# Moving the steps that decode weights within the first slots of a fused attention and MoE kernel: new units ahead of older ones, masks ahead of units, 1e-9 directly behind the exponentials

## The chip, the cores and the metric

The kernel runs on one core of one Trainium2 chip. The metric is the device time of one execution in microseconds (us); the median of three runs is compared. TensorE is PE in the profile, VectorE is DVE, ScalarE is ACT, GpSimd is POOL, and SyncE, which issues every transfer here, is SP.

## What is computed

The reference is attention that keeps the 32 largest scores of each row, and then four matrix products that mix what the heads give. There are 8 batches, 8 heads, 576 positions and 64 numbers per head.

```python
scores = scale * np.matmul(q, k.transpose(0, 1, 3, 2))
kth = np.partition(scores, -top_k, axis=-1)[..., -top_k:-top_k + 1]
mask = scores >= kth
scores = np.where(mask, scores, -1000000000.0)
scores = scores - np.max(scores, axis=-1, keepdims=True)
attn = np.exp(scores)
attn = attn / (np.sum(attn, axis=-1, keepdims=True) + 1e-09)
return np.matmul(attn, v).astype(np.float32)
...
a = x @ w1
b = x @ w2
h = a * b @ w3
return (h @ w_out).astype(np.float32)
```

w3 and w_out are folded into one matrix at the start, so what remains per token is x times w1, x times w2, their product, and that times the folded matrix.

## The kernel before

**Slots.** Attention is cut into 144 slots, 18 for each batch: 128 queries of two heads make a slot. A slot needs scores on PE, the 32 largest values of each row on DVE (four MAX8 rounds with MATCH_REPLACE8 between them), the mask, the exponentials, their sum, the division, a transposition and the product with v. The slots are pipelined by an order written out by hand: pass p of the main loop makes the scores of slot p+1, the largest values of slot p, the weights of slot j = p-1 (mask, exponentials, 1e-9, reciprocal, division) and the product with v of slot m = p-2. Every instruction is kept in the order of the program on its engine.

**The weights of one slot.** `edges_of` (POOL) makes the threshold of slot j from the values that DVE found. `mask` is for each of two heads a Relu on ACT and a subtraction on POOL, which the profile shows as `pab<-s,edge` and `pab<-s,pab`. `compare` (POOL, `over`) notes a number for a check at the end. `exps` are two exponentials on ACT (`pab<-pab,edge`) that also write their sums. `enlarge` adds 1e-9 to the two sums on POOL (`sums<-sums`), `invert` takes their reciprocal on DVE (`sums<-sums`), and `normalise` multiplies on POOL (`pab<-pab,sums`).

**Weight units.** The matrices come in as 40 units of 512 KB each: eight of w_out, then sixteen of w3 and sixteen of w1 and w2, mixed. The words of a unit come in a tile `z`, and there are four such tiles, so the transfer of a unit waits until the last reader of the unit four before it is done. Decoding takes several steps on different engines: ACT writes `t<-z` and then `z<-z`; DVE combines them in `y<-t` (TENSOR_SCALAR) and `y<-t,y` (SCALAR_TENSOR_TENSOR, called the STT here); POOL adds `y<-y,z` or `wo<-y,z`, the last reader of z. In every second unit of w_out and of w3 the first step is a TENSOR_SCALAR `y<-z` on POOL, and DVE has the STT only. A unit of w1 or w2 has two steps more, `wh<-y` on ACT and `wl<-y,wh` on POOL. A unit of w3 gives PE four products `pf` for the folded matrix, and every second one a copy on ACT and a subtraction on DVE (`wf`).

**Turns.** A call of `warm` is a turn: every unit that is under way makes its next step, and in four of five turns (from the eleventh in every second one) one new unit is begun. Each pass has five turns, called the first to the fifth here: behind the second step of the largest values, behind the transposition, behind the second round, behind the third round, and at the end of the pass. In pass -1 only the fourth and the fifth are made. `prefetch(3)` keeps three transfers ahead of the unit begun.

**The MoE.** When a part of a batch (320 or 256 tokens) has passed all its slots, its products (`ab`, then `eo`) are queued and put between the slots' work on PE by `fill`, in three portions to a pass. `fill` first issues what evicts earlier products (`evict`). The first `ab` waits until the first half of w1 and w2 is decoded. Products that the passes leave over are made at the end.

The names in the profile leave the numbers of buffers out; nearly all instructions carry one line, L52, that of the helper which keeps the order.

Of the kernel before, what the change touches and what calls it, by code (L numbers as in the profile page):

```python
# [60 lines left out]
def attn_moe(ctx: ExitStack, tc: tile.TileContext, q, k, v, w1, w2, w3, w_out, out, flag, general):  # L61
# [45 lines left out]
    def fetch(src):  # L107

        z = z_p.tile([128, 1024], F32, tag="z", name="z")
        sp.dma_start(z.bitcast(I32), src)  # L110
        return z
# [49 lines left out]
    def weigh(n):  # L161
        while heavy and n:
            heavy.pop(0)()
            n -= 1
# [31 lines left out]
    def load_qk(b, part, hp):  # L196

        lo, n, _ = PARTS[part]
        qt = kq_p.tile([128, NA], F32, tag="q", name="qt")
        sp.dma_start(qt[:, :n], at(q, b, hp)[:, lo : lo + n])  # L200
        kt = kq_p.tile([128, S + 64], F32, tag="k", name="kt")
        sp.dma_start(kt, at(k, b, hp))
        return qt, kt

    def load_v(b, hp):

        vt = kq_p.tile([128, 11 * D], F32, tag="v", name="vt")
        sp.dma_start(vt, at(v, b, hp))
        return vt
# [22 lines left out]
    def new_s():  # L232
        return att_p.tile([128, 2, S], F32, tag="s", name="s", bufs=2)
# [40 lines left out]
    def edges_of(slot):  # L274
        top = tops[slot % len(tops)]
        edge = small.tile([128, 2, 2], F32, tag="edge", name="edge")
        pool.tensor_tensor(edge, top[:, :, 0:32:31], coef, op=ALU.mult)
        return edge

    def compare(slot):  # L280
        top = tops[slot % len(tops)]
        pool.tensor_tensor(over[:, 2 * slot : 2 * slot + 2], top[:, :, 31], top[:, :, 23], op=ALU.subtract)
# [15 lines left out]
    def new_weights():  # L298
        return att_p.tile([128, 2, S], F32, tag="pab", name="pab"), small.tile([128, 2], F32, tag="sums", name="sums")

    def mask(s, edge, pab, a):

        act.activation(pab[:, a, :], s[:, a, :], AF.Relu, bias=edge[:, a, 1:2], scale=-STEEP)
        pool.tensor_tensor(pab[:, a, :], s[:, a, :], pab[:, a, :], op=ALU.subtract)

    def exps(edge, pab, sums, a):
        p = pab[:, a, :]
        act.activation(p, p, AF.Exp, bias=edge[:, a, 0:1], scale=SCALE, accum_out=sums[:, a : a + 1])

    def enlarge(sums):  # L310
        pool.tensor_scalar(sums, sums, 1e-9, None, op0=ALU.add)
# [20 lines left out]
    def take_turned(tp, ro):  # L332
        pts = att_p.tile([128, 2, 512], F32, tag="pts", name="pts", bufs=1)
        act.copy(pts, tp)
        pr = att_p.tile([128, 128], F32, tag="pr", name="pr")
        act.copy(pr, ro[:, :128])
        return pts, pr
# [26 lines left out]
    def take_low(to, ov):  # L364
        for x, cols, n in to:
            dve.tensor_tensor(x[:, 1, cols], ov[:, n], x[:, 0, cols].bitcast(F32), op=ALU.subtract)
# [116 lines left out]
    qk, vts, ss, sts, edges, pabs, xts, lows = {}, {}, {}, {}, {}, {}, {}, {}  # L483
# [5 lines left out]
    def evict():  # L489
        while put_off:  # L490
            put_off.pop(0)()

    def fill(n):
        nonlocal spare
        evict()
        spare = spare + n if queue else 0
        while queue and spare > 0:
            cost = next(queue[0], None)
            if cost is None:
                queue.pop(0)  # L500
            elif not cost:
                spare = 0
            else:
                spare -= cost

    waiting = list(startup)
    fetched, going, turns = [], [], []

    def prefetch(n):
        while waiting and len(fetched) < n:  # L510
            src, step = waiting.pop(0)
            fetched.append((fetch(src), step))

    def warm(first=True):

        if p < 0 and not first:
            return
        turns.append(p)
        n = len(turns)
        if fetched and (n % 5 if n < 11 else n % 2) and len(going) < 5:  # L520
            z, step = fetched.pop(0)
            going.append(step(z))
        going[:] = [unit for unit in going if next(unit, "end") != "end"]
        prefetch(3)

    qk[units[0]] = load_qk(*units[0])
    prefetch(3)
    n_slots = len(slots)
    for p in range(-1, n_slots + 3):
        i, j, m = p + 1, p - 1, p - 2  # L530
        if i < n_slots:
            for u in units:
                if first[u] - 2 == i:
                    qk[u] = load_qk(*u)
                if first[u] == i:
                    vts[u] = load_v(u[0], u[2])
        finder = top32_steps(ss[p], *sts.pop(p), p) if 0 <= p < n_slots else iter(())
        if 0 <= j < n_slots:
            edges[j] = edges_of(j)
        next(finder, None)  # L540
        if m - 1 in lows:
            take_low(*lows.pop(m - 1))
            b, part, _ = slots[m - 1][0][0]
            if final[b, part] == m - 1:
                queue.append(moe_steps(b, part, [xts.pop((b, part, hp)) for hp in range(NHP)], put_off.append))
        next(finder, None)
        if p >= 0:
            warm()
        if 0 <= j < n_slots:
            pabs[j] = new_weights()  # L550
            for a in range(2):
                mask(ss[j], edges[j], pabs[j][0], a)
            compare(j)
        fill(SHARE[0])
        next(finder, None)
        if 0 <= m < n_slots:
            tp, ro = turn(pabs[m][0])
            pts, pr = take_turned(tp, ro)
        warm(False)
        if 0 <= j < n_slots:  # L560
            exps(edges[j], *pabs[j], 0)
            exps(edges[j], *pabs[j], 1)
        weigh(1)
        fill(SHARE[1])
        next(finder, None)
        warm(False)
        if i < n_slots:
            st = scores([qk[u] for u in slots[i][0]], slots[i][1])
            ss[i] = new_s()
            take_scores(ss[i], st, 0)  # L570
            sts[i] = st, take_scores(ss[i], st, 1)
        if 0 <= m < n_slots:
            us, t = slots[m]
            for u in us:
                if u not in xts:
                    xts[u] = new_x()
            ov = values([vts[u] for u in us], t, pts, pr, ro)
            lows[m] = places([xts[u] for u in us], t), ov
            take_high(*lows[m])
        if 0 <= j < n_slots:  # L580
            enlarge(pabs[j][1])
        next(finder, None)
        warm()
        next(finder, None)
        if 0 <= j < n_slots:
            invert(pabs[j][1])
            normalise(*pabs[j])
        weigh(8)
        fill(SHARE[2])
        for _ in finder:  # L590
            pass
        if 0 <= m < n_slots:
            del ss[m], pabs[m], edges[m]
        warm()
# [62 lines left out]
```

## Time and profile before

| what | value |
|---|---|
| median of three runs | 1267.78 us (1266.63 to 1267.8) |
| the profiled execution's own time | 1266.87 us |
| its span, first to last instruction | 1264.9 us |
| busy: PE, DVE, ACT, POOL | 96%, 90%, 75%, 69% of the span |
| mean granted TensorE clock | 0.991 of full speed |

The span is what the trace covers; the execution's own time is 2 us longer. Busy shares are means over the whole span, while the change is in its first fifth and in one POOL instruction of each slot. So the views to read are those cut by stage. Idle time of an engine stands in brackets in a timeline, with what ended it.

### The profile page before, as it was taken

The numbers are of one execution on the slowest core, as the hardware profiler recorded it, in microseconds if no ns is written. First come the engines' busy times: TensorE is split into PE (matmuls) and PEld (weight loads), VectorE is DVE, ScalarE is ACT, GpSimd is POOL, SyncE is SP. The second block draws the span as 40 slices with busy tenths as digits, with TensorE's granted clock in tenths as the row PEclk, the third lists the DMA queues.
The fourth block names the chain that finished last, engine by engine and source line by source line (L and its number), as shares of the span: only waits on it lengthen the run. The fifth ranks groups of instructions, "written<-read, shape, count | busy, mean of one in ns | idle before, by whom it ended". The sixth has DMA issues, their size and how long they took to land.

```text
span 1264.9 us, 29916 instructions
## 1 busy us (share of the span) xinstructions
PE 1209.7 (96%) x10513; PEld 1043.5 (82%) x10513; DVE 1135.0 (90%) x3968; ACT 943.4 (75%) x2025; POOL 872.4 (69%) x1213
## 2 busy tenths in 40 slices
PE   3788889999999999999999999999999999999998
PEld 1444568888888888888888888888888888888898
DVE  7897979999999999999999999999999999999910
ACT  5887877777777777777777777777777777777731
POOL 5887887676766767676766767676766767676731
PEclk9999989999999999999999999999999999999999
DMA  7533421202112121202112121202112111202000
GB/s 236 174 129 130 156 70 40 91 27 70 55 39 90 36 63 40 90 28 70 55 39 91 36 63 40 90 28 70 55 39 91 35 63 40 91 27 70 13 22 21
DMA packets 42803, 85.92 MB, mean 68 GB/s; under 512 B 4754, under 2 KB 21138, under 8 KB 42642
## 3 DMA queue, kind: packets, MB, share of 16 engines
q1 hardware_dynamic: 42642, 83.91, 20.6%
q8 instruction: 85, 1.39, 0.5%
q14 instruction: 76, 0.62, 0.2%
HBM read 74.45 MB, written 9.44 MB: 66 GB/s over the span
## 4 chain that ended last, share of the span: by engine, by line
PE 75%; POOL 10%; DVE 7%; ACT 4%; issue 3%; DMA 1%; SPq 0%; DVEq 0%; POOLq 0%; ACTq 0%
PE ab L52 27%; PE eo L52 15%; PE ro L52 12%; PE st L52 11%; PE tp L52 9%; POOL pab L52 5%; DVE w L52 3%; DVE top L52 2%; ACT pab L52 2%; PE pf L52 2%; POOL y L52 2%; POOL g L52 1%; DVE y L52 1%; POOL wl L52 1%; ACT pts L52 1%
## 5 line engine op out<-in xcount | busy, mean ns | idle before, releaser
L52 POOL TENSOR_TENSOR pab<-s,pab 128x576 f32<-128x576 f32 x288 | 404.8, 1427 | 121.9 <-ACT pab L52 121.9
L52 DVE MAX8 top<-w 128x8 f32<-128x192 f32 (+1 forms) x1152 | 478.5, 448 | 0.0
L52 PE MATMUL ab<-xf,wh 128*128 128x256 f32 (+1 forms) x2048 | 438.5, 302 | 10.1 <-DVE y L52 8.7
L52 PEld LDWEIGHTS ab<-xf,wh 128*128 128x128 f32 x2048 | 332.9, 189 | 21.6 <-DVE y L52 9.5
L52 ACT ACTIVATE pab<-s,edge 128x576 f32<-128x576 f32 x288 | 208.0, 769 | 176.6 <-POOL edge L52 176.6
L52 PE MATMUL ab<-xf,wl 128*128 128x256 f32 (+1 forms) x1024 | 307.4, 300 | 0.0
L52 DVE MATCH_REPLACE8 w<-top,w 128x192 f32<-128x192 f32 x864 | 289.7, 343 | 0.0
L52 POOL TENSOR_SCALAR pab<-pab,sums 128x576 f32<-128x576 f32 x288 | 212.6, 751 | 78.0 <-DVE sums L52 78.0
L52 ACT ACTIVATE pab<-pab,edge 128x576 f32<-128x576 f32 x288 | 223.1, 779 | 11.9 <-POOL pab L52 9.7
L52 PE MATMUL eo<-g,wf 128*128 128x256 f32 (+1 forms) x1536 | 231.6, 301 | 0.0
L52 PEld LDWEIGHTS eo<-g,wf 128*128 128x128 f32 x1536 | 208.5, 188 | 8.1 <-issue 7.5
L52 PEld LDWEIGHTS ab<-xf,wl 128*128 128x128 f32 x1024 | 193.4, 189 | 4.1 <-issue 4.1
L52 PE MATMUL st<-kt,qt 64*128 64x192 f32 (+3 forms) x1280 | 182.8, 435 | 9.8 <-DMA kt<-in_k 4.8
L52 ACT COPY pts<-tp 128x1024 f32<-128x1024 f32 x144 | 145.6, 1011 | 46.8 <-PE tp L52 44.3
L52 ACT COPY s<-st 128x768 f32<-128x768 f32 (+1 forms) x288 | 169.9, 646 | 5.8 <-PE st L52 5.8
L52 PE MATMUL tp<-ident,pab 128*128 128x128 f32 x1152 | 153.8, 278 | 14.2 <-DVE w L52 9.5
L52 PEld LDWEIGHTS st<-kt,qt 64*128 64x128 f32 (+1 forms) x1280 | 97.9, 178 | 83.7 <-issue 18.6
L52 DVE TENSOR_TENSOR w<-w,st 128x384 f32<-128x384 f32 x288 | 158.2, 549 | 4.9
L52 PE MATMUL ro<-pts,vt 128*64 128x128 f32 (+1 forms) x2560 | 161.2, 269 | 1.0 <-ACT pr L52 1.0
L52 DVE TENSOR_TENSOR w<-s,st 128x384 f32<-128x384 f32 x288 | 146.7, 551 | 14.0
L52 POOL TENSOR_TENSOR g<-whole,g 128x256 fp32r<-128x256 f32 (+1 forms) x128 | 103.3, 807 | 78.6 <-ACT g L52 78.6
L52 PEld LDWEIGHTS ro<-pts,vt 128*64 128x64 f32 x2560 | 127.5, 137 | 34.4 <-issue 24.2
(47 smaller groups left out, 1128.7 us busy)
## 6 DMA issues: line engine op xcount, KB each, us to landing
vt<-in_v SPq DMA_DIRECT2D x64, 352.0 KB, 3.2
kt<-in_k SPq DMA_DIRECT2D x64, 320.0 KB, 3.8
z<-in_w SPq DMA_DIRECT2D x32, 512.0 KB, 3.8
qt<-in_q SPq DMA_DIRECT2D x32, 160.0 KB, 3.2
out_t<-osb SPq DMA_DIRECT2D x32, 160.0 KB, 1.8
z<-in_wo SPq DMA_DIRECT2D x8, 512.0 KB, 5.2
qt<-in_q SPq DMA_DIRECT2D x32, 128.0 KB, 3.1
out_t<-osb SPq DMA_DIRECT2D x32, 128.0 KB, 1.7
```

Source lines behind the costliest of these rows:

```text
L52: ins = fn(*args, **kw)
```

## The change

Four things move; no instruction is added or taken away.

- In a turn, the unit begun makes its first step ahead of the next steps of the units under way; before it came behind them.
- In each pass the two masks and `compare` stand ahead of the first turn; before they stood behind it.
- `enlarge` stands directly behind the two exponentials of its slot; before it stood behind the second portion of the MoE, the third turn, the scores and the product with v.
- Pass -1 makes one turn instead of two, so one unit instead of two is begun ahead of slot 0, and every unit is begun one turn later.

```diff
         turns.append(p)
-        n = len(turns)
+        n, new = len(turns), None
         if fetched and (n % 5 if n < 11 else n % 2) and len(going) < 5:
             z, step = fetched.pop(0)
-            going.append(step(z))
+            new = step(z)
+            next(new)
         going[:] = [unit for unit in going if next(unit, "end") != "end"]
+        if new:
+            going.append(new)
         prefetch(3)
...
         next(finder, None)
-        if p >= 0:
-            warm()
         if 0 <= j < n_slots:
             pabs[j] = new_weights()
             for a in range(2):
                 mask(ss[j], edges[j], pabs[j][0], a)
             compare(j)
+        if p >= 0:
+            warm()
         fill(SHARE[0])
...
             exps(edges[j], *pabs[j], 1)
+            enlarge(pabs[j][1])
         weigh(1)
         fill(SHARE[1])
...
-        if 0 <= j < n_slots:
-            enlarge(pabs[j][1])
         next(finder, None)
-        warm()
+        if p >= 0:
+            warm()
```

The queues show it at three places. The number behind a name counts the tiles made; it differs between the two kernels for the same tile. First POOL in pass 1, around the masks of slot 0 (`pab<-s,pab`); `wo<-y,z` and `y<-y,z` are last steps of units, `y<-z` first steps. Before:

```order
L52 TENSOR_TENSOR wo_105<-y_168,z_138 128x512
L52 TENSOR_TENSOR edge_214<-top0_98,coef_93 128x4
L52 TENSOR_TENSOR y_195<-y_195,z_144 128x512
L52 TENSOR_SCALAR y_224<-z_170 128x512
L52 TENSOR_TENSOR pab_228<-s_131,pab_228 128x576 x2
L52 TENSOR_TENSOR over_96<-top0_98 128x2
L52 TENSOR_TENSOR wo_105<-y_206,z_159 128x512
L52 TENSOR_SCALAR sums_229<-sums_229 128x2
```

And now:

```order
L52 TENSOR_TENSOR edge_205<-top0_98,coef_93 128x4
L52 TENSOR_TENSOR pab_212<-s_131,pab_212 128x576 x2
L52 TENSOR_TENSOR over_96<-top0_98 128x2
L52 TENSOR_TENSOR wo_105<-y_169,z_138 128x512
L52 TENSOR_SCALAR y_232<-z_174 128x512
L52 TENSOR_TENSOR y_196<-y_196,z_149 128x512
L52 TENSOR_SCALAR sums_213<-sums_213 128x2
L52 TENSOR_TENSOR wo_105<-y_219,z_163 128x512
L52 TENSOR_SCALAR pab_212<-pab_212,sums_213 128x576 x2
L52 TENSOR_SCALAR y_286<-z_226 128x512
L52 TENSOR_TENSOR wo_105<-y_232,z_174 128x512
L52 TENSOR_TENSOR wo_105<-y_246,z_201 128x512
```

The last step of the fourth unit (the one that reads z_138) was ahead of the threshold and now stands behind both masks. Next ACT in the same pass, behind the masks' Relus. The seventh unit is the one of z_170 before and z_174 now, the eighth that of z_199 before and z_201 now. Before:

```order
L52 ACTIVATE pab_228<-s_131,edge_214 128x576 x2
L52 ACTIVATE t_241<-z_170 128x512
L52 ACTIVATE z_170<-z_170 128x512
L52 ACTIVATE t_245<-z_199 128x512
L52 ACTIVATE z_199<-z_199 128x512
L52 ACTIVATE pab_228,sums_229<-pab_228,edge_214 128x576 x2
L52 COPY s_270<-st_260 128x2x384
```

And now:

```order
L52 ACTIVATE pab_212,sums_213<-pab_212,edge_205 128x576 x2
L52 ACTIVATE t_247<-z_201 128x512
L52 ACTIVATE z_201<-z_201 128x512
L52 ACTIVATE t_252<-z_174 128x512
L52 ACTIVATE z_174<-z_174 128x512
L52 COPY s_267<-st_257 128x2x384
```

The eighth unit's first step now stands ahead of the seventh's, and both ahead of the copies of the scores. Last POOL in pass 8, where before three steps of units stood between the threshold and the masks:

```order
L52 TENSOR_TENSOR edge_943<-top1_99,coef_93 128x4
L52 TENSOR_TENSOR wl10_108<-y_878,wh1_102 128x512
L52 TENSOR_TENSOR y_921<-y_921,z_781 128x512
L52 TENSOR_SCALAR y_954<-z_832 128x512
L52 TENSOR_TENSOR pab_958<-s_793,pab_958 128x576 x2
L52 TENSOR_TENSOR over_96<-top1_99 128x2
L52 TENSOR_SCALAR sums_959<-sums_959 128x2
```

And now:

```order
L52 TENSOR_TENSOR edge_935<-top1_99,coef_93 128x4
L52 TENSOR_TENSOR pab_943<-s_787,pab_943 128x576 x2
L52 TENSOR_TENSOR over_96<-top1_99 128x2
L52 TENSOR_SCALAR y_972<-z_852 128x512
L52 TENSOR_TENSOR wl10_108<-y_885,wh1_102 128x512
L52 TENSOR_TENSOR y_928<-y_928,z_810 128x512
L52 TENSOR_SCALAR sums_944<-sums_944 128x2
```

The masks follow the threshold at once, the begun unit's `y<-z` is the first of the three steps, and all three stand between the masks and `sums`. On PE the queue from the first `ab` on is the same row by row in both kernels; ahead of it only some `pf` products stand a pass later.

## Rows read from the trace of the kernel before

**Rows 1.** Busy time by stretch: us, PE, PEld, DVE, ACT, POOL, clock, DMA share, GB/s.

```profile
10.00:40.34 30.34, 12.87 (x69) 6.21 (x69) 29.80 (x90) 21.85 (x41) 23.85 (x27) 1.00 0.64 206
40.34:123.89 83.55, 72.22 (x401) 38.75 (x402) 72.53 (x219) 63.27 (x125) 67.16 (x81) 0.94 0.43 143
123.89:182.58 58.69, 48.61 (x299) 35.27 (x298) 52.48 (x159) 48.09 (x95) 52.98 (x60) 0.91 0.38 124
200.00:1200.00 1000.00, 998.30 (x9116) 890.13 (x9114) 954.08 (x3417) 774.76 (x1686) 698.52 (x999) 1.00 0.18 55
```

**Rows 2.** All waits of PE from 200 to 1200 us: total, times, longest.

```profile
PE tp L52 <- DVE w L52: 0.7, 4, 0.2
```

**Rows 3.** Timeline of DVE: slot starts (`w<-s,st`) and the waits named.

```profile
8.24 0.69 DVE L52 TENSOR_SCALAR y<-t 128x512 int32<-128x512 int32 x1 [8.24 <-ACT t L52]
...
9.57 1.01 DVE L52 TENSOR_TENSOR w<-s,st 128x384 f32<-128x384 f32 x2
...
20.24 1.01 DVE L52 TENSOR_TENSOR w<-s,st 128x384 f32<-128x384 f32 x2
...
30.57 1.02 DVE L52 TENSOR_TENSOR w<-s,st 128x384 f32<-128x384 f32 x2
...
40.34 1.02 DVE L52 TENSOR_TENSOR w<-s,st 128x384 f32<-128x384 f32 x2
...
49.93 0.69 DVE L52 SCALAR_TENSOR_TENSOR y<-t,y 128x512 int32<-128x512 int32 x1 [2.47 <-POOL y L52]
...
108.08 0.69 DVE L52 TENSOR_SCALAR y<-t 128x512 int32<-128x512 int32 x1 [2.30 <-ACT t L52]
...
120.57 0.69 DVE L52 SCALAR_TENSOR_TENSOR y<-t,y 128x512 int32<-128x512 int32 x1 [2.46 <-ACT xf L52]
...
123.89 1.01 DVE L52 TENSOR_TENSOR w<-s,st 128x384 f32<-128x384 f32 x2
...
182.58 1.02 DVE L52 TENSOR_TENSOR w<-s,st 128x384 f32<-128x384 f32 x2
```

**Rows 4.** Groups of POOL and ACT, 20 to 190 us: busy, mean ns, idle before.

```profile
L52 POOL TENSOR_TENSOR pab<-s,pab 128x576 f32<-128x576 f32 x30 | 41.8, 1416 | 7.2 <-ACT pab L52 7.2
L52 POOL TENSOR_TENSOR y<-y,z 128x512 int32<-128x512 int32 x32 | 41.5, 1298 | 1.3 <-ACT z L52 1.1
L52 POOL TENSOR_SCALAR pab<-pab,sums 128x576 f32<-128x576 f32 x28 | 20.6, 749 | 9.7 <-DVE sums L52 9.7
L52 POOL TENSOR_TENSOR wl<-y,wh 128x512 fp32r<-128x512 f32 x16 | 20.5, 1280 | 4.7 <-ACT wh L52 4.7
L52 ACT ACTIVATE t<-z 128x512 f32<-128x512 f32 x34 | 22.1, 650 | 7.0 <-DVE y L52 6.0 <-DMA z<-in_wo 1.0
L52 ACT ACTIVATE pab<-s,edge 128x576 f32<-128x576 f32 x30 | 21.6, 767 | 5.5 <-POOL edge L52 5.5
```

**Rows 5.** Timelines of ACT and POOL in the first two slots.

```profile
6.50 1.18 ACT L52 COPY s<-st 128x768 f32<-128x768 f32 x2 [4.49 <-PE st L52]
...
17.83 1.28 POOL L52 TENSOR_TENSOR wo<-y,z 128x512 int32<-128x512 int32 x1 [1.67 <-DVE y L52]
...
23.39 0.64 ACT L52 ACTIVATE t<-z 128x512 f32<-128x512 f32 x1 [1.00 <-DMA z<-in_wo]
...
31.48 0.20 POOL L52 TENSOR_TENSOR edge<-top,coef 128x4 f32<-128x4 f32 x1
```

**Rows 6.** The chain that ended last, first slots: start, us, what.

```profile
14.87 3.77 DMA z<-in_wo
```

**Rows 7.** Transfers over the whole run: KB each, median us to landing.

```profile
z<-in_wo SPq DMA_DIRECT2D x8, 512.0 KB, 5.2
```

**Rows 8.** Timeline of POOL ahead of DVE's wait that ends at 49.93.

```profile
46.71 1.28 POOL L52 TENSOR_TENSOR wl<-y,wh 128x512 fp32r<-128x512 f32 x1
47.94 1.30 POOL L52 TENSOR_TENSOR y<-y,z 128x512 int32<-128x512 int32 x1
...
49.21 0.69 POOL L52 TENSOR_SCALAR y<-z 128x512 f32<-128x512 f32 x1
```

## The prediction

> **What bounds the kernel now.** I read the stretches first, to see which engine is full where. From 200 to 1200 us PE is busy 998.3 of 1000 us at full clock [rows 1], and in all that time it waits 0.7 us for anything [rows 2]. So in steady slots PE sets the pace, and no other engine's order matters. Since the queue of PE is the same row by row from the first `ab` on, the end comes as much later or earlier as PE leaves the start later or earlier. Ahead of that PE idles 17.5 us up to 40.34 us, 11.3 us up to 123.89 and 10.1 us up to 182.58, and what it waits for is the slots' work on the other engines. The view to read next is therefore DVE's timeline, where each first `w<-s,st` marks the start of a slot [rows 3]: slot 0 at 9.57, slot 1 at 20.24, slot 2 at 30.57, slot 3 at 40.34, slot 10 at 123.89, slot 15 at 182.58. DVE idles 0.5 us in slots 0 to 2, 11.0 us in slots 3 to 9, and 6.2 us in slots 10 to 14 [rows 1]. The bound of the first 40 us is DVE's own work; then three engines take turns, POOL being busy 53.0 of 58.7 us in slots 10 to 14, more than any other.
>
> **How I work the change out.** Each engine takes its queue in the new order; a step starts when its engine is free and what it reads is there. I walked slots 0 to 15 so by hand. A threshold takes 0.2 us, a Relu 0.7, a mask 1.4, the division of both heads 1.5, an addition that ends a unit 1.3, a `wl` 1.25, a `t` or a `z` about 0.6 [rows 4, 5]; a unit takes 1.33 us on DVE (9.57 less 8.24), one with the STT alone half of that [rows 3].
>
> **Slot 0: earlier.** One unit less is ahead of it. DVE begins with the scores when the first copy is made, about half of the 1.18 us behind 6.50 [rows 5], so at 7.2 instead of 8.24: 1.0 us of idle time is gone. The slot holds the same two whole and two half units as before and so lasts the same 10.67 us; slot 1 starts at 17.9 instead of 20.24, but one unit, 1.3 us, is still to be done later.
>
> **Slots 1 and 2: later.** The fourth unit's last step was done at 19.1, ahead of the masks [rows 5]; now it stands behind them. The threshold can start at 17.4 (half a unit ahead of slot 1); 0.2 for it, 0.7 for the Relu, 2.8 for the masks, 0.2 for the check's number and 1.3 for the addition end at 22.6. Only then is the tile free for the eighth unit, and the transfer takes 3.8 us as in the chain [rows 6]: 26.4, where ACT had it at 23.39 [rows 5]. [...] The trace has 3.77 here and a median of 5.2 for these eight units [rows 6, 7], so I stay with 3.8 and take 5.2 as the upper bound. ACT comes to the eighth unit's `t` with nothing else to do at 22.6, and waits; behind it stand the seventh unit's `t`, whose data are there, and the scores of slot 2. DVE runs dry at 26.2, and gets the seventh unit's `t` three steps behind 26.4, at 28.2: 2.0 us lost. [...] The loss is larger on POOL. The division of slot 0 waits for the reciprocal, which stands behind this on DVE, until 30.9; the division (1.5), a first step (0.65) and two additions (2.6) then stand ahead of the next threshold, which starts at 35.6, not at 31.48 [rows 5]. In pass 2 the Relus are ahead of the new unit's `t`: that is ready at 35.6 + 0.2 + 1.4 + 0.6 = 37.8, and DVE wants it at 34.7, 3.1 us lost; a second `t`, behind the exponentials, costs 0.8. Slot 3 so starts at about 44.8 with the same eleven units begun: **+4.5 us** (0 if nothing of it is on the path, +5.9 with a transfer of 5.2 us).
>
> **Slots 3 to 9: earlier.** Here are the waits that the new order removes. DVE's 2.47 us that end at 49.93 are for a unit's first step on POOL, which stood behind a `wl` and an addition of older units [rows 8]; now it stands ahead of both, 2.5 us sooner. The 2.46 us that end at 120.57 are of the same kind: the wait is put down to ACT, but the STT reads the `y<-z` of POOL. The 2.30 us at 108.08 are a `t` behind exponentials whose masks had to stand behind units [rows 3]; now the masks are ahead of them. Against this POOL loses cover. Between the threshold and the first mask lies a Relu (0.7 us and the way to and fro, about 0.75) with nothing behind which to hide it. And `enlarge` now waits for the exponentials while `wl` and additions of the third turn stand behind it; in slots 3, 6 and 9 I find POOL waiting 2.2 to 2.8 us so. The walk leaves 6.9 of the 11.0 us of DVE's idle time: -4.1 us, and -1.3 us for the unit that is still behind. **-5.4 us** (0 if the new waits on POOL eat it all, -11.0 if all idle time goes).
>
> **Slots 10 to 14: later.** POOL sets the pace here, and what was put off at the start is paid: one unit more, 1.3 + 1.25 us, of which some 0.2 comes back, because the reciprocal no longer waits behind a third-turn step: **+2.3 us** (0 to 2.5). Behind slot 15 the units are over and PE is full again.
>
> **The rest at nothing.** In the steady slots `enlarge` only changes place with one subtraction of the MoE, on a POOL that is busy 698.5 of 1000 us, and PE waits for none of it [rows 1, 2]. Without that cover it would cost the wait for the exponentials in each slot. In the pf products that come a pass later PE has room: it is busy 72.2 of 83.55 us in slots 3 to 9. [...]
>
> **The sum:** 4.5 - 5.4 + 2.3 = +1.4 us. Against the profiled execution's 1266.87 us that is 1268.3; its time is 0.9 us under the median 1267.78, so as a median **1269.2 us**. A measurement here can tell about 0.2%, 2.5 us, from no change, so this counts as no change.
>
> **Rivals.** *The early loss does not come.* If the eighth unit's data are there when ACT reaches them at about 22.6 us, and the threshold of slot 1 is no later than before, the first term is -1.0 instead of +4.5; -1.0 - 5.4 + 2.3 = -4.1, 1263.7 us. For it: in the trace before, waits for z of 1.00 us at 23.39 and more cost DVE nothing [rows 3, 5]. Against it: the addition that frees the tile really stands 3.7 us of threshold, Relu and masks later. *POOL becomes the bound.* POOL is busy 80% and 90% in slots 3 to 9 and 10 to 14 [rows 1]; if its waits for the exponentials and the Relus reach DVE in every slot, the second term is 0 and not -5.4: +6.8, 1274.6 us. It decides once POOL's slot, some 10.6 us of work (52.98 us in five slots) and 1.5 to 3 of waits, is longer than DVE's slot, which the walk has at 10 to 12. *Nothing reaches the end.* If PE were full already when slot 15 starts, a delay of one or two us would be swallowed: 1267.8. Against it: PE idles 10.1 us in slots 10 to 14 [rows 1], so it has no backlog to live on.
>
> **How the numbers follow.** The forecast, within 3 us of its time, together with the third rival, has 0.47; the early loss staying away 0.28; POOL as the bound 0.25. Below 1265.2 us lies nearly all of the second and little else: faster 0.28. Above 1270.3 lies the third and a part of the forecast's own spread: slower 0.30; no change 0.42. The range reaches past 1263.7 and to 1274.6, and by one more us of transfer (5.2 instead of 3.8) and of removed idle time on each side: 1261.5 to 1275.5. The likeliest case alone is 1266.5 to 1272.
>
> **What would show it.** DVE's first row at about 7.2; a wait of ACT for z of 3 us or more near 23 to 26; slot 3 at 44 to 45; no wait of DVE for a `y<-z` of POOL afterwards; waits of POOL's `sums` for ACT of 2 us in single slots; slot 10 near 122.7 and slot 15 near 184. Slot 3 near 40 would prove the second term's gain unopposed, and slot 10 behind 126 the rival on POOL. The forecast is wrong above all if the transfers or the copies of the scores start at other times than the walk has them, since each slot inherits the delay of the one ahead.

## The result: slower

The changed kernel takes **1278.57 us** (median of four runs, 1278.0 to 1279.37) against 1267.36 us for the kernel before, measured beside it (four runs), a ratio of 1.0089 with a 95% interval of 1.0075 to 1.0103. That is 11.2 us more, where 1.4 more were forecast, and above the range. The profiled execution took 1278.02 us over a span of 1275.9.

### The profile page after: what moved, and what is told of

Its sections match the earlier page's. It is cut to its first block, busy times and chain, and to the rows that moved or that the text cites. A ratio compares the mean times of both kernels' runs of the same rounds, so it can differ in the third digit from the quotient of the medians.

```text
span 1275.9 us, 29886 instructions
## 1 busy us (share of the span) xinstructions
PE 1210.4 (95%) x10513; PEld 1046.1 (82%) x10513; DVE 1139.4 (89%) x3968; ACT 942.0 (74%) x2025; POOL 871.8 (68%) x1213
## 4 chain that ended last, share of the span: by engine, by line
PE 88%; POOL 5%; ACT 3%; issue 2%; DVE 2%; DMA 1%; SPq 0%; ACTq 0%; POOLq 0%; DVEq 0%
PE ab L52 33%; PE eo L52 17%; PE ro L52 15%; PE st L52 12%; PE tp L52 9%; POOL pab L52 2%; PE pf L52 2%; POOL y L52 2%; ACT pab L52 1%; DVE y L52 1%; ACT t L52 1%; POOL wl L52 1%; DVE top L52 0%; ACT pts L52 0%; DVE w L52 0%
## 5 line engine op out<-in xcount | busy, mean ns | idle before, releaser
L52 PE MATMUL st<-kt,qt 64*128 64x192 f32 (+3 forms) x1280 | 186.3, 441 | 22.6 <-DVE w L52 9.8
L52 PE MATMUL tp<-ident,pab 128*128 128x128 f32 x1152 | 151.1, 274 | 7.2 <-DVE w L52 7.1
L52 POOL TENSOR_SCALAR sums<-sums 128x2 f32<-128x2 f32 x144 | 30.9, 214 | 167.5 <-ACT pab L52 166.9
```

Source lines behind the costliest of these rows:

```text
L52: ins = fn(*args, **kw)
```

## The profile after

The stretches of the kernel after, cut at its own starts of slots 3, 10 and 15; they answer to [rows 1].

```profile
core 0: us, PE busy (x) PEld busy (x) DVE busy (x) ACT busy (x) POOL busy (x), PEclk, DMA share, GB/s
10.00:45.20 35.20, 13.74 (x63) 7.06 (x61) 28.53 (x87) 21.20 (x40) 24.09 (x28) 0.84 0.53 171
45.20:132.34 87.14, 70.86 (x395) 37.96 (x395) 72.12 (x218) 62.47 (x124) 64.26 (x77) 0.91 0.41 133
132.34:198.99 66.65, 49.86 (x288) 34.69 (x290) 54.25 (x161) 48.32 (x95) 56.10 (x63) 0.90 0.36 117
200.00:1200.00 1000.00, 1000.00 (x9162) 894.72 (x9161) 960.49 (x3432) 777.70 (x1696) 701.88 (x1005) 1.00 0.18 56
```

Slots 3 to 9 take 87.14 us and not 83.55, slots 10 to 14 take 66.65 and not 58.69. DVE idles 15.0 us in the first of these stretches (87.14 less 72.12), where it had 11.0. From 200 us on PE is as good as full in both kernels (1000.0 and 998.3 of 1000 us). So the whole loss is made ahead of 200 us.

DVE's timeline of the kernel after, its slot starts and its longest early waits, for [rows 3].

```profile
6.76 1.02 DVE L52 TENSOR_TENSOR w<-s,st 128x384 f32<-128x384 f32 x2 [6.76 <-ACT s L52]
...
17.43 1.01 DVE L52 TENSOR_TENSOR w<-s,st 128x384 f32<-128x384 f32 x2
...
28.20 0.69 DVE L52 SCALAR_TENSOR_TENSOR y<-t,y 128x512 int32<-128x512 int32 x1 [2.53 <-ACT t L52]
...
31.71 1.02 DVE L52 TENSOR_TENSOR w<-s,st 128x384 f32<-128x384 f32 x2
...
37.89 0.69 DVE L52 SCALAR_TENSOR_TENSOR y<-t,y 128x512 int32<-128x512 int32 x1 [2.93 <-ACT t L52]
...
45.20 1.01 DVE L52 TENSOR_TENSOR w<-s,st 128x384 f32<-128x384 f32 x2
```

A loss in the start is best counted in what PE still has to do at 200 us, since PE is as good as full behind that. Two rows, first of the kernel before and then of the one after:

```profile
200.00:1290.00 1090.00, 1057.31 (x9605) 947.90 (x9603) 963.40 (x3448) 792.99 (x1730) 713.97 (x1021) 1.00 0.17 52
```

```profile
200.00:1290.00 1090.00, 1070.53 (x9744) 963.04 (x9742) 980.35 (x3500) 805.00 (x1759) 725.44 (x1037) 1.00 0.17 53
```

PE has 13.2 us more to do. But of the span behind 200 us it idles 7.6 us before (1264.9 less 200 less 1057.31) and 5.4 us after. So the start loses 13.2 us and the steady slots, with the drain, give 2.2 back: 11.0 us of span. The table keeps these two numbers for each kernel, in the order in which the runs are told.

| kernel | median us | ratio to before, 95% | PE busy behind 200 us | PE idle behind 200 us |
|---|---|---|---|---|
| before | 1267.36 | 1 | 1057.3 | 7.6 |
| after | 1278.57 | 1.0075 to 1.0103 | 1070.5 | 5.4 |
| a_masks_back | 1264.21 | 0.9968 to 0.9986 | 1055.6 | 5.4 |
| a_enl_back | 1285.04 | 1.0122 to 1.0153 | 1076.7 | 7.9 |
| a_new_back | 1280.80 | 1.0088 to 1.0119 | 1074.0 | 5.6 |
| a_turn_back | 1277.49 | 1.0063 to 1.0090 | 1069.9 | 7.4 |
| b_masks | 1282.46 | 1.0110 to 1.0141 | 1071.8 | 8.9 |
| b_enl | 1262.61 | 0.9955 to 0.9980 | 1054.4 | 5.5 |
| b_enl_new | 1261.30 | 0.9940 to 0.9967 | 1053.7 | 5.4 |
| a_weigh_late | 1278.08 | 1.0073 to 1.0104 | 1070.0 | 5.7 |
| a_relu_first | 1266.62 | 0.9988 to 1.0006 | 1059.0 | 5.6 |
| a_mask_one | 1269.45 | 1.0010 to 1.0030 | 1063.6 | 5.6 |
| a_wf_later | 1279.47 | 1.0085 to 1.0116 | 1072.1 | 5.4 |
| bn_relu | 1261.98 | 0.9948 to 0.9976 | 1053.9 | 5.5 |
| a_check_first | 1278.45 | 1.0069 to 1.0097 | 1071.1 | 5.5 |
| a_edge_early | 1275.05 | 1.0043 to 1.0070 | 1068.8 | 5.6 |
| a_exps_first | 1273.52 | 1.0036 to 1.0063 | 1065.3 | 5.4 |
| bn_exps | 1268.25 | 1.0000 to 1.0018 | 1059.6 | 5.8 |
| a_ways | 1269.47 | 1.0010 to 1.0028 | 1060.4 | 5.4 |
| bn_edge | 1259.55 | 0.9928 to 0.9955 | 1052.3 | 5.4 |

A name that begins with a is the kernel after with one thing altered (a_ways: three), b the kernel before with one or two of the edits, bn the kernel b_enl_new with one thing more. The kernel before was measured anew beside each group of runs (medians of 1266.37 to 1267.36 us), and the ratios are to that. By their intervals a median is good to 1 or 2 us, so differences of about 1 us between two kernels are no finding. The two columns on PE are of one profiled execution each.

## The theories

The trace after showed a chain that the forecast did not have. The chain of work that ended last, in slot 4 of the kernel after (start, length, what):

```profile
58.23 0.17 POOL edge L52
58.41 0.02 issue
58.43 0.78 ACT pab L52
59.21 0.07 issue
59.28 0.65 POOL pab L52
59.93 0.72 issue
60.65 1.42 POOL pab L52
62.07 0.15 POOL over L52
62.22 1.25 POOL y L52
63.48 0.04 issue
63.52 1.13 PE pf L52 x2
64.64 2.04 PE st L52 x8
```

Threshold, Relu and two masks stand in a row ahead of a unit's addition `y`, and PE's one `pf` for it ahead of the next scores `st`. **Loop theory:** the masks ahead of the first turn are the loss, and that `pf` passes it on. **Cover theory** (one half of the forecast's rival on POOL): the early 1e-9 makes POOL wait for the exponentials. **Early starvation:** the late transfer of the eighth unit is the loss. A fourth place is the unit put off from pass -1.

## Experiments: each edit taken back

**a_masks_back.**

```diff
+        if p >= 0:
+            warm()
         if 0 <= j < n_slots:
             pabs[j] = new_weights()
...
             compare(j)
-        if p >= 0:
-            warm()
```

> The changed kernel, with the masks behind the units' first turn again as before the change; the other three edits stay. Loop theory (the masks ahead of the units put the addition that a unit ends with behind them; the one product of the weights that stands ahead of the scores in PE's queue waits for it, and the scores, ACT's copy and the next slot of DVE wait behind): most of the loss goes, 1268 to 1272 us, and PE's waits for y at pf shrink from 17.6 us to under 8. Cover theory (POOL's sum of the small number now waits for the exponentials): little goes, 1275 to 1279. Early starvation of z (the first three slots carry the loss): 1273 to 1275, since the 4.9 us at the start of slot 3 go, for the eighth unit's tile is then free as early as before.

Measured 1264.21 us: 14.4 us go, more than any theory said, and the kernel is faster than before. PE has 14.9 us less left at 200 us. The masks are the loss, and more than all of it. PE's waits for `y` at `pf` fall from 17.6 to 8.5 us up to 230 us, not to under 8 as the loop theory had it. DVE's starts of slots 3, 10 and 15 in this kernel:

```profile
42.32 1.01 DVE L52 TENSOR_TENSOR w<-s,st 128x384 f32<-128x384 f32 x2
...
121.20 1.01 DVE L52 TENSOR_TENSOR w<-s,st 128x384 f32<-128x384 f32 x2
...
183.65 1.02 DVE L52 TENSOR_TENSOR w<-s,st 128x384 f32<-128x384 f32 x2 [2.41 <-ACT s L52]
```

So slots 3 to 9 take 78.9 us and slots 10 to 14 62.5, against 87.1 and 66.7 with the masks ahead.

**a_enl_back.**

```diff
             exps(edges[j], *pabs[j], 1)
-            enlarge(pabs[j][1])
...
             take_high(*lows[m])
+        if 0 <= j < n_slots:
+            enlarge(pabs[j][1])
```

> The changed kernel, with the small number added to the sums behind the scores and the high halves again; the other three edits stay. Cover theory: POOL's waits at the sums (12.1 us before 230 us) are most of the loss, 1268 to 1272 us. Loop theory: those waits only add to the chain from masks to y to pf, 2 to 4 us go, 1274 to 1277. Early starvation: nothing goes, 1278.

Measured 1285.04 us, 6.5 us more. The cover theory falls: the early sum gains, in the profiled executions 6.2 us in the start and 2.5 us of PE's idle time behind 200 us, which no theory had.

**a_new_back.**

```diff
-            new = step(z)
-            next(new)
+            going.append(step(z))
         going[:] = [unit for unit in going if next(unit, "end") != "end"]
-        if new:
-            going.append(new)
```

> The changed kernel, with the new unit's first step behind the older units' steps again. Loop theory: a new unit's y then again stands behind wl and additions, but these come sooner, so the time changes by at most 2 us either way, 1276 to 1280. Early starvation: the eighth unit's t no longer stands ahead of the seventh's in ACT's queue while it waits for its transfer; 2 to 4 us go, 1274 to 1276. Cover theory: nothing, 1278.

Measured 1280.80 us, 2.2 us more, though its interval overlaps that of after; PE has 3.5 us more to do at 200 us. Slot 3 now starts at 43.76 and not 45.20, so the early loss became smaller, and nothing of it reached the end. Early starvation is not what sets the end. As this edit also takes the early first steps from the later slots, it doesn't price the early loss by itself.

**a_turn_back.**

```diff
-        if p >= 0:
-            warm()
+        warm()
```

> The changed kernel, with the two turns of the units ahead of slot 0 again two and not one. If the unit that is put off from there is what is paid in slots 10 to 14, with the tiles of z that come free later, 2 to 5 us go, 1273 to 1276. Loop theory: the chain from masks to y to pf is the same in each slot, so about 1.3 us go for the one unit less that is left, 1276 to 1278. Cover theory: nothing, 1278.

Measured 1277.49 us, 1.1 us less, an interval that overlaps that of after. The unit put off is a small part here. (Its 7.4 us of idle time hold a single wait of 1.8 us, of `st` for `pts`, between 198 and 212 us.)

## Experiments: one edit alone, and the way by PE

**a_weigh_late.**

```diff
-        weigh(1)
         fill(SHARE[1])
...
             take_high(*lows[m])
+        weigh(1)
```

> The changed kernel, all four edits kept, with the one product of the weights that stands ahead of the scores in PE's queue put behind the scores, the values and the high halves. If this product passes the late y on to the scores (loop theory by PE's queue): at least half of the 14 us that the masks cost go, 1266 to 1272 us, and no ACT wait of s for st of over 2 us follows a wait of pf. If the masks cost by POOL's own idle time (POOL waits 21.7 us for pab of ACT before 230 us, 12.9 with the masks back): less than 3 us go, 1275 to 1280; it may also lose, since the products come later.

Measured 1278.08 us, by the ratio the same as after. PE's waits for `y` at `pf` fell from 17.6 to 7.8 us up to 208 us, and slots 3 to 9 took 83.8 us and not 87.1. But slots 10 to 14 took 68.1 and not 66.7, slot 15 took 10.0 and not 8.8, and PE has nearly as much left at 200 us (1070.0 against 1070.5). So the half of the loop theory that named PE's queue falls as the price of the masks: the product is on the chain, and moving it gains nothing by the end. What takes the gain back behind slot 9 was not found.

**b_masks.**

```diff
-        if p >= 0:
-            warm()
         if 0 <= j < n_slots:
...
             compare(j)
+        if p >= 0:
+            warm()
```

> The kernel before, with the masks ahead of the units' first turn and no other edit. If the masks alone are the loss: 1280 to 1284 us, by the 14.4 us that taking them back gave in the changed kernel. If it is the masks together with the early sum (the sum and the masks crowd POOL between threshold and division): under 1274. With the sum late, the changed kernel took 1285.0, so the sum of the parts speaks for the first.

Measured 1282.46 us, 1.26% or 16 us over before: the masks alone do it, whatever the other edits.

**b_enl.**

```diff
             exps(edges[j], *pabs[j], 1)
+            enlarge(pabs[j][1])
...
-        if 0 <= j < n_slots:
-            enlarge(pabs[j][1])
```

> The kernel before, with the small number added directly behind the exponentials and no other edit. In the steady slots PE idled 1.7 us between 200 and 1200 us with the sum late and 0 with it early, so 2 us should go there: 1265 us. If POOL loses its cover in the first 200 us (13 waits of the sums for the exponentials), 3 to 5 us come on top of that: 1268 to 1270. If the sum is worth what it is in the changed kernel (6.5 us): 1261.

Measured 1262.61 us, a gain of 0.33% or 4.2 us; in the profiled executions PE has 2.9 us less to do at 200 us and 2.1 us less idle time behind it.

**b_enl_new.**

```diff
-            going.append(step(z))
+            new = step(z)
+            next(new)
         going[:] = [unit for unit in going if next(unit, "end") != "end"]
+        if new:
+            going.append(new)
```

> The kernel before, with the early sum and the new unit's first step ahead, that is the changed kernel with masks and turn taken back. It tells what the one turn less ahead of slot 0 is worth where the masks are behind: if the turn costs what it does in the changed kernel (about 1 us), 1263; if the seventh and eighth unit's z are then late, as in the changed kernel, 1267; with no effect of the turn, 1264.

Measured 1261.30 us. The interval overlaps that of b_enl, so the 1.3 us of the new unit's first step are not clear of the noise. From it to a_masks_back only pass -1's turn differs: one turn less costs 2.9 us by the medians where the masks are behind, and 1.9 us of PE's work left at 200 us. In the kernel after it was 1.1 us and not clear of the noise. So the change can be read as four steps in this order, by the ratios (a per cent of before is 12.7 us): early sum -0.33%, new unit first -0.13%, one turn less +0.23%, masks ahead +1.12%.

## Experiments: why the masks cost

POOL stands at the mask until ACT has made the Relu. POOL's waits between 36 and 205 us, kernel before and kernel after (waited for, us in all, times, longest):

```profile
POOL pab L52 <- DVE sums L52: 10.3, 12, 2.4
POOL pab L52 <- ACT pab L52: 8.7, 10, 1.3
```

```profile
POOL pab L52 <- ACT pab L52: 19.9, 14, 3.5
POOL sums L52 <- ACT pab L52: 11.1, 9, 2.6
POOL pab L52 <- DVE sums L52: 3.5, 5, 1.2
```

11.2 us more at the mask looks like the loss. The next five kernels ask whether it is, and what makes the Relu late.

**a_relu_first.** `mask` is cut into its Relu and its subtraction.

```diff
+                relu(ss[j], edges[j], pabs[j][0], a)
+        if p >= 0:
+            warm()
+        if 0 <= j < n_slots:
+            for a in range(2):
+                cutoff(ss[j], pabs[j][0], a)
             compare(j)
-        if p >= 0:
-            warm()
```

> The changed kernel, where the Relus stay ahead of the units' first turn on ScalarE, and only the masks and the check's number go back behind it on GpSimd. Standing theory (GpSimd stands at the mask while the Relu is late, with steps of units behind it that could run; 14 waits of 0.9 to 3.5 us between 36 and 205 us, 20.0 us in all): the loss goes as with the masks back, 1262 to 1266 us, and a little below that kernel's 1264.2, since the Relu is made during the units' steps. If the order on ScalarE is what costs (the Relus ahead of the units' t): little goes, 1274 to 1279.

Measured 1266.62 us: 12.0 of the 14.4 us go. POOL's queue carries the loss; the order on ACT has the other 2.4.

**a_mask_one.**

```diff
             pabs[j] = new_weights()
-            for a in range(2):
-                mask(ss[j], edges[j], pabs[j][0], a)
-            compare(j)
+            mask(ss[j], edges[j], pabs[j][0], 0)
         if p >= 0:
             warm()
+        if 0 <= j < n_slots:
+            mask(ss[j], edges[j], pabs[j][0], 1)
+            compare(j)
```

> The changed kernel with one head's Relu and mask ahead of the units' first turn and the other head's behind it. Standing theory: the wait for the first Relu is paid as before the split, and the second Relu now stands behind the units' steps on ScalarE, so almost nothing goes, 1275 to 1281 us. If what counts is how much GpSimd work stands ahead of the units (2.8 us of masks in each slot): half of the 14 us goes, 1270 to 1273.

Measured 1269.45 us: 9.1 us go, more than either theory said, and far from that of a lost wait. The waits at the mask stay (16.7 us in the same stretch, 19.9 in after), and yet nearly two thirds of the loss are gone. So here the loss follows how much mask stands ahead of the units and not the wait at the mask. By which readers it is paid, this run doesn't tell.

**a_wf_later.**

```diff
         if i == 1:
+            yield
             cut = slice(f * DM, (f + 1) * DM)
```

> The changed kernel, where a unit that ends in the folded weights makes its copy wf one turn later, so that ScalarE no longer waits for the products of PE with the next Relu behind that copy. Standing theory with the wf copy as what makes the Relu late: the four waits of 3.5, 2.8, 3.0 and 1.8 us at the mask fall to 0.9, 7.5 us go, 1270 to 1273 us. If the long waits at the mask come from elsewhere, or the loss is the 0.9 us of every slot: 1276 to 1280.

Measured 1279.47 us. The long waits at the mask went as expected, and nothing came of it:

```profile
POOL sums L52 <- ACT pab L52: 15.0, 10, 3.0
POOL pab L52 <- ACT pab L52: 12.6, 14, 1.0
POOL pab L52 <- DVE sums L52: 6.8, 6, 2.3
```

Of 7.3 us less at the mask 7.2 came back at the sum and at the division. That sum of waits was no price; POOL now waits at another place.

**a_check_first.** The check's number between the Relus and the masks.

```diff
             for a in range(2):
-                mask(ss[j], edges[j], pabs[j][0], a)
+                relu(ss[j], edges[j], pabs[j][0], a)
             compare(j)
+            for a in range(2):
+                cutoff(ss[j], pabs[j][0], a)
```

> The changed kernel with the check's number, 0.2 us on GpSimd, between threshold and first mask and not behind the masks. Uncovered-Relu theory: the wait at each mask falls from 0.89 to about 0.7 us, and 16 times 0.2 is 3 us: 1275 to 1276. Displacement theory: nothing, 1278 to 1279, since the units' steps stand behind the same work.

Measured 1278.45 us, the same as after. Again the waits at the mask shrink (19.9 to 17.2 us in the same stretch) and those at the sum grow (11.1 to 13.7).

**a_edge_early.**

```diff
-        if 0 <= j < n_slots:
-            edges[j] = edges_of(j)
...
         for _ in finder:
             pass
+        if 0 <= p < n_slots:
+            edges[p] = edges_of(p)
```

> The changed kernel with the threshold of a slot made one turn earlier: on GpSimd it stands ahead of the units' last turn of the pass, so that this turn's steps lie between threshold and first mask. The masks stay ahead of the first turn. Uncovered-Relu theory (0.9 us in each of 16 slots): 10 us or more of the 14 go, 1264 to 1269 us, and the waits of 0.89 us at the mask are gone. Displacement theory (the first turn's steps come 2.8 us later): under 4 us go, 1275 to 1279.

Measured 1275.05 us: 3.5 us go. But the run tells less than was hoped: the wait at the mask is gone in four of 14 slots and as long or longer in the others, 18.3 of the 19.9 us, since the Relu now stands behind the last turn's steps on ACT. It doesn't take the wait away, so it can't price it. What speaks against the wait as the price are a_mask_one, a_wf_later and a_check_first.

**a_exps_first.** Where the sum waits, ACT's queue shows why. ACT and then POOL in slot 6 of the kernel after:

```profile
87.16 0.63 ACT L52 ACTIVATE t<-z 128x512 f32<-128x512 f32 x1
87.73 0.67 ACT L52 ACTIVATE z<-z 128x512 int32<-128x512 uint16 x1
88.30 0.99 ACT L52 COPY pts<-tp 128x1024 f32<-128x1024 f32 x1
...
89.35 0.63 ACT L52 ACTIVATE t<-z 128x512 f32<-128x512 f32 x1
89.93 0.67 ACT L52 ACTIVATE z<-z 128x512 int32<-128x512 uint16 x1
90.50 0.76 ACT L52 ACTIVATE pab<-pab,edge 128x576 f32<-128x576 f32 x1
```

```profile
86.67 2.79 POOL L52 TENSOR_TENSOR pab<-s,pab 128x576 f32<-128x576 f32 x2 [0.89 <-ACT pab L52]
89.42 0.19 POOL L52 TENSOR_TENSOR over<-top 128x2 f32<-128x2 f32 x1
92.20 0.21 POOL L52 TENSOR_SCALAR sums<-sums 128x2 f32<-128x2 f32 x1 [2.59 <-ACT pab L52]
```

The masks are done at 89.46, but the exponentials stand behind two turns' `t` and `z`, and POOL idles 2.59 us. In slot 9 the masks themselves come back this way. POOL there:

```profile
123.43 2.80 POOL L52 TENSOR_TENSOR pab<-s,pab 128x576 f32<-128x576 f32 x2 [0.89 <-ACT pab L52]
...
126.34 1.29 POOL L52 TENSOR_TENSOR y<-y,z 128x512 int32<-128x512 int32 x1
129.90 0.21 POOL L52 TENSOR_SCALAR sums<-sums 128x2 f32<-128x2 f32 x1 [2.27 <-ACT pab L52]
```

The addition stands behind the masks and is done at 127.63. ACT's `wh<-y` waits 1.43 us for it and starts at 127.66, the exponentials stand behind `wh`, and POOL waits for them until 129.90.

```diff
-        warm(False)
         if 0 <= j < n_slots:
             exps(edges[j], *pabs[j], 0)
             exps(edges[j], *pabs[j], 1)
+        warm(False)
+        if 0 <= j < n_slots:
             enlarge(pabs[j][1])
```

> The changed kernel with the exponentials ahead of the units' second turn on ScalarE, so that they no longer stand behind that turn's t and wh; the sum stays where it is. If the late exponentials are what the masks cost (the wh of the second turn waits for the first turn's addition, which is now behind the masks; GpSimd's waits at the sums are 11.1 us before 208 us): 5 us or more go, 1268 to 1273. If not: 1276 to 1281, and DVE waits longer for the second turn's t.

Measured 1273.52 us: 5.0 us go, and the waits at the sum fall to 3.4 us, though DVE's waits for `t` rise from 15.4 to 21.2 us up to 208 us. Part of the loss is that the masks came early and their readers did not.

**a_ways.** The edits of a_exps_first, a_edge_early and a_weigh_late together.

```diff
-        warm(False)
...
+        warm(False)
...
-        weigh(1)
...
+        weigh(1)
...
+            edges[p] = edges_of(p)
```

> The changed kernel, masks ahead of the units' first turn, with three edits together: the exponentials ahead of the second turn on ScalarE, the threshold one turn earlier on GpSimd, the product of the weights behind the scores on PE. If the three are separate costs: 5.0 + 3.5 + 0.5 = 9 us go, 1269 to 1271 us. If they are ways beside each other, each of which holds the slot when another is gone: clearly more than 9, 1264 to 1268. If the loss is in the units' steps behind the masks whatever their readers are: no more than with the exponentials alone, 1272 to 1275.

Measured 1269.47 us: 9.1 us go, as the sum of the three had it (of which a_weigh_late's 0.5 is within the noise). So they add up and are not ways beside each other. It also means that 9.1 of the 14.4 us go with both masks still ahead of the first turn: what their place costs hangs on where the threshold and the exponentials stand. Some 5 us of the 14.4 stay with the masks ahead; slot 16 starts at 197.65 and not at 192.70 as in a_masks_back, with 1.5 us of that lost by slot 3. Which reader of the units' steps carries these was not found.

## Experiments: faster versions

**bn_relu.** The cut of a_relu_first on b_enl_new.

```diff
+                relu(ss[j], edges[j], pabs[j][0], a)
         if p >= 0:
             warm()
...
+                cutoff(ss[j], pabs[j][0], a)
```

> The kernel before with the early sum and the new unit's first step ahead (1261.3 us), and besides with the Relus on ScalarE ahead of the units' first turn, while the masks stay behind it on GpSimd. Standing theory: GpSimd's waits for the Relus (9 waits, 9.5 us before 208 us) shrink to under 3 us, of which GpSimd is the last in about half of the slots: 1256 to 1260 us. If ScalarE's order costs (the units' t later, on which DVE waits 16.0 us): 1262 to 1266.

Measured 1261.98 us, no gain: the waits at the mask shrank only from 9.5 to 7.4 us, and those at the sum grew from 12.4 to 14.3.

**bn_exps.** The edit of a_exps_first on b_enl_new.

```diff
-        warm(False)
         if 0 <= j < n_slots:
             exps(edges[j], *pabs[j], 0)
             exps(edges[j], *pabs[j], 1)
+        warm(False)
```

> The fastest kernel so far (the kernel before with the early sum and the new unit's first step ahead, 1261.3 us), with the exponentials ahead of the units' second turn on ScalarE. There they wait for the masks anyway, which are behind the first turn: the second turn's t then stand behind that wait, and DVE, which waits 16.0 us for t before 208 us, waits longer: 1262 to 1268. If the earlier exponentials shorten GpSimd's 12.4 us at the sums: 1257 to 1260.

Measured 1268.25 us, 7.0 us more. The same edit that gives 5.0 us with the masks ahead costs 7.0 with the masks behind: there ACT waits for the masks in front of the exponentials (9.7 us before 208 us, 4.4 without the edit), the second turn's `t` stand behind, and DVE waits 26.1 us for `t`, not 16.0.

**bn_edge.** The edit of a_edge_early on b_enl_new.

```diff
+        if 0 <= p < n_slots:
+            edges[p] = edges_of(p)
```

> The fastest kernel so far (the kernel before with the early sum and the new unit's first step ahead, 1261.3 us), with the threshold one turn earlier on GpSimd. There the Relu has the first turn as a cover already, so little is left: 1259 to 1262. If GpSimd then waits for the slot's last maximum of VectorE, with the last turn's steps behind it: 1262 to 1266.

Measured **1259.55 us**, the lowest median of all, ratio to before 0.9941 (0.9928 to 0.9955). The 1.8 us under b_enl_new are not clear of the noise; the 0.6% under before are. The windows of bn_edge show PE with 5.0 us less to do at 200 us than the kernel before:

```profile
200.00:1290.00 1090.00, 1052.32 (x9595) 946.54 (x9593) 963.55 (x3444) 791.86 (x1730) 711.39 (x1019) 1.00 0.17 52
```

## Why the prediction was wrong

**Slots 0 to 2: right.** The term said +4.5 us at slot 3, and 4.9 were measured (45.20 against 40.34). Its parts stand in the trace too. ACT and DVE waited for the eighth unit as the walk had it:

```profile
26.36 0.63 ACT L52 ACTIVATE t<-z 128x512 f32<-128x512 f32 x1 [4.52 <-DMA z<-in_wo]
...
27.48 0.61 ACT L52 ACTIVATE t<-z 128x512 f32<-128x512 f32 x1
```

The data were there at 26.36 (forecast 26.4), the seventh unit's `t` followed only then, DVE went on at 28.20 (28.2), and the next threshold came at 35.60 (35.6). Where the transfer was bounded at 3.8 to 5.2 us, the lower end was right: it took 3.91 us on the chain. With the masks back slot 3 starts at 42.32, so 2.9 of the 4.9 us are the masks', as the walk had it with the addition behind them. That this lag carries to the end is less sure: a_new_back had 1.4 us less of it and did not end earlier.

**Slots 3 to 9: the step that failed.** It said -5.4 us and the stretch became 3.6 us longer, 9.0 us off. The term counted three waits that the masks and the new first steps remove, 2.3 to 2.5 us each, and for the masks a price of 0.75 us per slot of Relu without cover, inside a walk in which a step's readers come when it is done. The waits that were removed came back as others: DVE idles 15.0 us there, not the 6.9 that the walk left. What the walk left out here, though it had it in slots 1 and 2, is that 3.0 us of masks and check now stand between a threshold and all units' steps of the first turn, in every slot. Taking half of the masks away from there gave 9.1 us back, all of them 12.0, and the Relus with them 14.4. With masks and Relus behind the turn again the stretch takes 78.9 us, 4.7 less than before, and DVE idles 7.6 us (69.45 busy of 77.00 between 45 and 122 us), near the -5.4 and the 6.9 of the walk. So with the other three edits alone the stretch comes out close to the term. That is partly luck, since the term had worked the masks in, with one of its three waits (2.30 us) and with the price of the Relus. The masks, which the term had among the gains, cost 8.3 us in these slots. Through which steps is known in part: 9.1 of the 14.4 us went by moving the exponentials and the threshold as well, the rest stays open. The forecast's other edits were on the gaining side: the early sum gives 0.33%, the new unit first 0.13%, the second not clear of the noise.

**Slots 10 to 14: mis-sized, half by the same.** The term had +2.3 us for one unit more on POOL; the stretch took 8.0 us longer. With the masks back it is 3.8 us longer (62.45), so 4.2 us are the masks' again. The unit more was put too low: b_enl_new, which differs from a_masks_back in pass -1's turn alone, takes 57.1 us here (122.51 to 179.57), 5.4 less. With the turn left out slot 3 starts 1.6 us later too, but slots 3 to 9 are 2.9 us shorter and slot 15 is 2.1, so slot 16 starts 2.0 us later.

**The rest at nothing: wrong by 2.2 us, to the better.** PE's 998.3 of 1000 us with 0.7 us of named waits [rows 1, 2] were read as a full engine. With the early sum it is 1000.0 (after, a_masks_back, a_new_back and b_enl; a_turn_back has 998.1), and behind 200 us PE idles 5.4 and not 7.6 us. Where the 1.0 us without a named wait came from is not shown. In each pair that differs in the sum alone (a_enl_back and after, before and b_enl) the difference is 2.1 to 2.5 us.

**The pf products at nothing: not settled.** PE was on the chain, and its waits for `y` at `pf` rose from 2.8 us before to 17.6 up to 230 us. Yet a_weigh_late, which took more than half of them away, gained nothing that is clear of the noise.

**The rivals.** That POOL becomes the bound was the rival nearest to the time, 1274.6 us, and it had the right engine; the sign named for it, slot 10 behind 126 us, came with 132.34. Its reason was half wrong: the waits at the sum that it feared came with an edit that gains, and a_wf_later and a_check_first moved waits of POOL to and fro at no gain. That the early loss stays away, or that nothing reaches the end, fell with slot 3 at 45.20 and 13.2 us more left for PE at 200 us. Even the upper bounds of the three terms together (5.9 + 0 + 2.5 = 8.4 us) give only 1276.2 us, itself above the stated range: no term had room for what the masks cost.

## What to carry to other kernels

Where several engines work in order, a step moved ahead must be priced by what now stands behind it in every slot, and by where its readers stand, not by the wait that it removes; try it with half of the step to see whether the price follows its length. A sum of waits at one place need not be a gain to be had: cut it and see whether it comes back at the next hand-over. Moves of a producer and of its reader belong together, and the same move of the reader alone gained 5 us here or lost 7, by where its producer stood.

## What the runs showed of the hardware that was not expected

PE's granted clock in the start was lower than before: a mean of 0.84 between 10 and 45.20 us and 0.90 to 0.91 until 198.99, against 1.00, 0.94 and 0.91 [rows 1]. It was 0.50 from 40 to 50 us, and 0.70 in the 10 us ahead of that, in which PE was busy 3.36 us:

```profile
20.00:30.00 10.00, 6.07 (x20) 2.37 (x12) 7.36 (x25) 4.87 (x10) 5.70 (x7) 1.00 0.59 194
30.00:40.00 10.00, 3.36 (x17) 1.91 (x17) 6.93 (x23) 4.17 (x7) 8.07 (x10) 0.70 0.43 132
40.00:50.00 10.00, 6.32 (x35) 4.31 (x31) 9.04 (x26) 8.06 (x17) 7.76 (x11) 0.50 0.40 129
```

A mean busy share doesn't tell the clock here: the kernel before had 1.00 with PE busy 12.87 of 30.34 us, the one after 0.84 with 13.74 of 35.20. In the kernel after a `tp` product took 424 ns from 40 to 50 us (mean of 8) and 272 ns from 200 to 1200 us, at 1.00. The lower clock added little to PE's own work: ahead of 200 us PE was busy 12.6 us less than before, and had 13.2 us more to do behind it, so over the whole span its busy time is only some 0.7 us more. What such slower products added to the chains ahead of 200 us is not shown. The windows of the kernel before, then of the one after:

```profile
0.00:200.00 200.00, 152.39 (x910) 95.61 (x911) 171.57 (x521) 150.44 (x295) 158.43 (x193) 0.95 0.44 146
```

```profile
0.00:200.00 200.00, 139.83 (x771) 83.05 (x772) 159.08 (x470) 137.03 (x267) 146.34 (x176) 0.90 0.43 142
```
